# Batch 0's second half: sums a unit later, the next pair's clusters with precedence, its preparation two units sooner

## The chip, the cores and the metric

The kernel runs on one core of a Trainium2 chip. Its engines work side by side, each through a queue of its own: TensorE (PE in the profile, PEld for its weight loads), VectorE (DVE), ScalarE (ACT), GpSimd (POOL) and the sync engine (SP), which issues most transfers. The metric is the device time of one execution in microseconds; the reference point is the median of three runs.

## What is computed

Attention over clusters, followed by a feed-forward layer with a squared ReLU. B, H, S, D = 4, 8, 768, 64; 16 clusters; the model width is 512, the hidden width 2048.

```python
q_assign = np.argmax(np.einsum('bhsd,hcd->bhsc', q_n, c_n), axis=-1)
k_assign = np.argmax(np.einsum('bhsd,hcd->bhsc', k_n, c_n), axis=-1)
mask = q_assign[:, :, :, None] == k_assign[:, :, None, :]
scores = scale * np.matmul(q, k.transpose(0, 1, 3, 2))
scores = np.where(mask, scores, -1000000000.0)
...
attn = attn / (np.sum(attn, axis=-1, keepdims=True) + 1e-09)
return np.matmul(attn, v)
# then, with the heads side by side as x (3072 x 512):
h = x @ w_in
r = np.maximum(h, 0.0)
return ((r * r) @ w_out)
```

A query attends to the keys of its own cluster only.

## The kernel before

**Units.** Heads go in pairs (16 pairs, four in a batch), queries in two halves of 384, keys in blocks of 128. A unit is one pair, one half and two key blocks; there are 96. Batch 0 takes its four pairs with the first half of the queries (units 0 to 11) and then the same four pairs with the second half (units 12 to 23, three for a pair). From unit 24 on, each pair of batches 1 to 3 has its six units in one piece. `TWOS` is 12, `HP` is 4, `NCH` is 6.

**A unit.** `scores` multiplies keys and queries into two PSUM tiles `sc`, and for batch 0 adds a penalty from the one-hot clusters; ScalarE takes the exponential (line 466). From pair 4 on, VectorE masks the result by comparing cluster numbers `qid` and `ids` (line 470). `times_v` multiplies by the values into `av`, for two units together at odd units. In batch 0's first half TensorE itself sums the exponentials; in the second half and later GpSimd adds them up in `acc` (lines 480, 482).

**The end of a pair and half.** `add_up` multiplies `acc` by a constant on TensorE into `sm` (a tile of the pool `ps_f`, which has two banks and serves logits, turned logits, sums and the feed-forward alike), takes the reciprocal `r` on VectorE (line 551), sends it to DRAM as `far_r` and brings it back spread over the partitions as `rb`, all through the sync queue. One unit later `finish` multiplies `av` by `rb` into `xT` (line 570) and so releases the `av` bank; there are two of these.

**Preparation.** `prep(pair)` is a list of steps, three of which are taken in each unit. For pairs 4 and up it is: bring the words of q and k back turned (`turn_words`), split the next pair's words (`split_words`, two calls), `logits`, `route` (which turns the logits into `lt` on TensorE and finds each row's cluster on VectorE, lines 340 to 349), and `spread`, which sends the cluster numbers to all partitions. For pair 4 the two halves of its own words are split by the main loop, in units 12 and 15; its preparation begins in unit 18 (line 764), and its first scores are in unit 24.

**Beside it.** In units 0 to 23 `round_weights` rounds 32 tiles of the feed-forward weights in pieces that ScalarE, VectorE and GpSimd take in turn (lines 150 to 166): one tile in most units, two in every third. Four staging tiles `w_raw` are loaded through the sync queue as they come free. The feed-forward of batch 0 (`ffn`, lines 584 and 597) is cut into single matmuls that fill TensorE between the attention's own; it begins at the end of the first half. The feed-forward of batches 1 to 3 runs after unit 95.

**Order.** The program is traced unit by unit; each engine's instructions are put in order by the time at which a model finds them ready and by precedence, where earlier traced goes first. `tc.high_priority(offset=n)` treats what it encloses as if it had been traced n places earlier. `tc.issue_after` puts instructions behind one that is named. On the chip each engine then works through its written order.

Of the kernel before, what the change touches and what calls it, by code (L numbers as in the profile page):

```python
# [25 lines left out]
def kernel(  # L26
# [14 lines left out]
    NCH = S // P  # L41
# [4 lines left out]
    HP = H // 2  # L46
# [54 lines left out]
    def load_qk(pair):  # L101
        if pair >= NG:
            return
        b, hp = divmod(pair, HP)
        raw[pair] = []
        for name, src in (("q_raw", q), ("k_raw", k)):
            t = loads.tile([P, NCH, 2 * D], F32, name=name, tag="qk")
            for e in range(2):
                (nc.scalar if pair == 0 and e else nc.sync).dma_start(
                    t[:, :, D * e : D * (e + 1)],  # L110
                    src[b, 2 * hp + e].rearrange("(p j) d -> p j d", p=P),
                )
            raw[pair].append(t)

    def load_v(pair):
        b, hp = divmod(pair, HP)
        raw_v[pair] = loads_v.tile([P, 2, NCH, D], F32, name="v_raw")
        nc.sync.dma_start(
            raw_v[pair], v[b, 2 * hp : 2 * hp + 2].rearrange("h (p j) d -> p h j d", p=P)
        )  # L120
# [16 lines left out]
    def load_weights(i):  # L137
        raw_w[i] = wstage.tile([P, NW, 2], U32, name="w_raw")
        nc.sync.dma_start(raw_w[i], weights[i][1])
# [129 lines left out]
    def split_words(pair, which):  # L269
        if which == 0:  # L270
            words[pair] = dram.tile([2 * NCH, P, 2, 2 * D], U16, name="words")
        flat = loads.tile([P, NCH, 2, 2 * D], U16, name="flat", tag="qk")
        src = raw[pair][which].bitcast(U16).rearrange("p c (d two) -> p c two d", two=2)
        half = NCH // 2
        with tc.issue_after(last_exp[0]):
            for cols in (slice(0, half), slice(half, NCH)):
                nc.scalar.copy(out=flat[:, cols], in_=src[:, cols])
        nc.sync.dma_start(
            words[pair][NCH * which : NCH * (which + 1)].rearrange("c p two d -> p c two d"),
            flat,  # L280
        )
        if which == 1:
            raw.pop(pair)
            load_qk(pair + 1)
# [22 lines left out]
        nc.scalar.copy(out=lgs[pair], in_=lg)  # L307

    def route(pair):
        with tc.high_priority(offset=2000) if pair < HP else ExitStack():  # L310
            number(pair)

    def number(pair):
# [95 lines left out]
    def prep(pair):  # L409
        if pair < HP:  # L410
            return [
                lambda: turn(pair, 0), lambda: turn(pair, 1), lambda: turn(pair, 2),
                lambda: logits(pair), lambda: route(pair),
                lambda: turn_onehot(pair, 0), lambda: turn_onehot(pair, 1),
            ]

        split = [lambda i=i: split_words(pair + 1, i) for i in range(2 if pair + 1 < NG else 0)]
        first, second = split or (None, None)
        return [
            lambda: turn_words(pair), None, None, first, None, None,  # L420
            lambda: logits(pair), None, lambda: route(pair), second, None, None,
            None, None, lambda: spread(pair),
        ]
# [9 lines left out]
    def first_half(pair, h):  # L433
        return pair < HP and h == 0
# [63 lines left out]
    def wide(pair, h):  # L498

        return (pair, h) == (HP - 1, 0)  # L500

    def times_v(pair, h, c):
        if c == 0:
            av[pair, h] = ps_av.tile([P, TB], F32, name="av", tag="av")
            if first_half(pair, h):
                n = TB if wide(pair, h) else TB // 2
                sums[pair, h] = ps_av.tile([P, n], F32, name="sm", tag="av")
        t = ex.pop((pair, h, c))
        products = [
            dict(  # L510
                out=av[pair, h][D * e : D * (e + 1)], lhsT=raw_v[pair][:, e, c + i],
                rhs=t[:, 2 * i + e], start=(c + i == 0), stop=(c + i == NCH - 1),
            )
            for i in range(2) for e in range(2)
        ]
        if first_half(pair, h):
            for i in range(2):
                one = [
                    ones_products(
                        sums[pair, h], wide(pair, h), e, t[:, 2 * i + e], c + i == 0, c + i == NCH - 1  # L520
                    )
                    for e in range(2)
                ]
                products += [p for both in zip(*one) for p in both]
        together(products, 4000)
# [211 lines left out]
    TWOS = HP * NCH // 2  # L737
# [17 lines left out]
    def behind_first(u, what=last_logits):  # L755
        return tc.issue_after(what[0]) if u == 0 else ExitStack()

    def next_pair(u):

        pair, h, c = units[u]  # L760
        if c == 0 and pair + 1 < NG and h == 0 and (pair + 1) not in qkT:
            if pair + 1 < HP or pair >= HP:
                return pair + 1
        if c == 0 and h == 1 and pair == HP - 2:
            return HP
        return None

# [10 lines left out]
    for _ in range(AHEAD):  # L778
        load_weights(next(loaded))
    added = []  # L780
    v_next = 0

    def ends(halves):
        for pair, h in halves:
            b, hp = divmod(pair, HP)
            finish(pair, h)
            if hp == HP - 1 and (b, h) in PLAIN:
                fill.append(ffn(b, h))

    for u in range(len(units) + 2):  # L790
        if u < len(units):
            pair, h, c = units[u]
            if (p := next_pair(u)) is not None:
                ahead.extend(prep(p))
            if u in (HP * NCH // 2, HP * NCH // 2 + 3):

                split_words(HP, int(u > HP * NCH // 2))
            if c == 0 and u + 3 < len(units) and units[u + 3][0] not in raw_v:
                load_v(units[u + 3][0])

            with behind_first(u):
                scores(pair, h, c)

        ends(added)
        added.clear()
        if u < TWOS:
            ready = u - 1
        elif u == TWOS or u % 2 or u >= len(units):
            ready = u
        complete = []  # L810
        while v_next < min(ready, len(units)):
            pair, h, c = units[v_next]
            times_v(pair, h, c)
            v_next += 1
            if c == NCH - 2:
                complete.append((pair, h))
        for pair, h in complete:
            with tc.high_priority(offset=1000) if pair < HP else ExitStack():
                add_up(pair, h)
            if h == 1:  # L820
                for d in (qkT, ids, qid):
                    d.pop(pair)
            if h == 1 or pair < HP:
                raw_v.pop(pair)
            if wide(pair, h):
                with tc.high_priority(offset=1000):
                    ends([(pair, h)])
            else:
                added.append((pair, h))

        rounding += 4
        while rounding >= 3:
            rounding -= 3
            i = next(to_round, None)
            if i is not None:
                with tc.issue_after(last_exp[0]):
                    round_weights(i)
                if (i := next(loaded, None)) is not None:
                    load_weights(i)
            elif not later:  # L840
                early.close()
                for name, bufs in (("xT", 5), ("out", 2)):
                    later[name] = keep.enter_context(
                        tc.tile_pool(name=name + "_late", bufs=bufs, side="right",
                                     reuse_waits="tile")
                    )
        share = 0
        if u % 2 == 0 or not TWOS < u < len(units):
            n = 2 if TWOS < u < len(units) else 1
            share = max(0, left[0] - RESERVE) * sum(map(density, range(u, u + n)))  # L850
            share //= max(1, sum(map(density, range(u, ENDS))))
        goal = left[0] - share

        for i in range(3):
            if i == 2:
                fill_steps(share * 2 // 3)
            if ahead:
                with behind_first(u, masked if i else last_logits):
                    (ahead.pop(0) or int)()
        fill_steps(left[0] - goal)  # L860
# [235 lines left out]
```

## Time and profile before

| what | value |
|---|---|
| time, median of three runs | 995.92 us (994.25 to 997.6) |
| profiled span | 992.5 us |
| attention with batch 0's feed-forward | up to some 550 us |
| feed-forward of batches 1 to 3 | the rest |
| TensorE busy from 73.7 to 182 us (units 12 to 25) | 97.6 us |
| VectorE, ScalarE, GpSimd busy in the same stretch | 74.4, 59.9, 64.6 us |
| mean granted TensorE clock | 0.995 of full speed |

A row of the timeline has the start in us, the duration in us (of a merged run of instructions the stretch it covers), the engine, the line of the kernel, the operation, the tiles written and read, shapes, and the count; in brackets stands how long the engine was idle before it and what ended that. A line such as L91 is a helper's (`together`), so the tile tells which product it is: `sc` scores, `av` values, `sm` sums, `lg` logits, `lt` turned logits, `ph` and `po` feed-forward. Matmul ends are modelled, so durations of groups are taken from start to start.

### The profile page before, as it was taken

How to read it: one execution, taken by the hardware profiler on the slowest of the kernel's cores; microseconds unless marked ns; L12 is line 12 of the kernel's file. 1: busy time of each engine (PE TensorE's matmuls, PEld its weight loads, DVE VectorE, ACT ScalarE, POOL GpSimd, SP SyncE). 2: the span in 40 equal slices, each digit the busy share in tenths (PEclk: the TensorE clock that was granted, in tenths of full speed). 3: DMA queues.
4: the chain of work that ended last, by engine and by line, in shares of the span. 5: the costliest groups of instructions: out<-in, count | busy, mean ns of one | idle time of the engine just before them, and what ended most of it. 6: DMA issues, size and time to landing. Idle time of an engine off the chain costs nothing.

```text
span 992.5 us, 12014 instructions
## 1 busy us (share of the span) xinstructions
PE 963.3 (97%) x4455; PEld 552.3 (56%) x4455; DVE 563.4 (57%) x913; ACT 315.5 (32%) x510; POOL 374.4 (38%) x277
## 2 busy tenths in 40 slices
PE   7998989999999999999899999999999999999997
PEld 4543434343444444444343555888655888556886
DVE  5767584765566656666765855533465531556331
ACT  5885664444445455554232111000111000111000
POOL 1336574555565565655556332001331002231000
PEclk9999998999999999999999999999999999999999
DMA  9654655345554445544310000000000000000000
GB/s 259 192 179 143 180 167 120 96 107 129 123 128 123 113 115 111 138 106 99 88 38 17 20 0 1 1 22 22 21 1 0 11 22 27 7 0 1 22 22 24
DMA packets 127576, 74.32 MB, mean 75 GB/s; under 512 B 90907, under 2 KB 118935, under 8 KB 127511
## 3 DMA queue, kind: packets, MB, share of 16 engines
q1 hardware_dynamic: 125798, 73.06, 28.0%
q8 instruction: 37, 0.61, 0.2%
q10 hardware_dynamic: 1712, 0.43, 0.2%
q14 instruction: 29, 0.23, 0.1%
HBM read 48.07 MB, written 15.86 MB: 64 GB/s over the span
## 4 chain that ended last, share of the span: by engine, by line
PE 79%; DVE 5%; issue 5%; DMA 5%; POOL 3%; SPq 1%; ACT 1%; ACTq 0%; POOLq 0%; DVEq 0%
PE bank L707 22%; PE bank L676 22%; PE po L597 7%; PE ph L584 6%; PE sc L91 5%; PE sc L94 5%; PE av L91 4%; PE av L94 4%; DMA rb<-far_r 2%; POOL acc L482 2%; POOL w_in L166 1%; DVE ex L470 1%; PE sm L91 1%; DVE w_raw L162 1%; DVE r L551 1%
## 5 line engine op out<-in xcount | busy, mean ns | idle before, releaser
L482 POOL TENSOR_TENSOR acc<-acc,ex 128x768 f32<-128x768 f32 x112 | 205.0, 1830 | 124.9 <-DVE ex L470 99.7
L470 DVE SCALAR_TENSOR_TENSOR ex<-qid,ids,sc 128x384 f32<-128x384 bf16 x288 | 157.6, 607 | 62.2 <-ACT sc L466 40.7
L466 ACT ACTIVATE sc<-sc 128x768 f32<-128x768 f32 x144 | 108.6, 793 | 162.7 <-PE sc L94 136.7
L94 PE MATMUL sc<-qkT 64*128 64x384 f32 x576 | 153.1, 504 | 0.9
L94 PE MATMUL av<-ex,v_raw 128*64 128x384 f32 x576 | 136.8, 494 | 0.0
L646 DVE TENSOR_TENSOR g<-bank,g 128x384 f32<-128x384 f32 x144 | 77.8, 555 | 81.6 <-PE bank L676 80.5
L665 POOL TENSOR_TENSOR w_s<-w_in 128x256 f32<-128x256 f32 x24 | 18.2, 760 | 278.5 <-PE bank L707 162.0
L584 PE MATMUL ph<-xT,w_in 128*128 128x384 f32 x256 | 94.6, 511 | 0.7 <-DVE xT L570 0.7
L707 PE MATMUL bank<-w_out,g 128*128 128x256 f32 x432 | 95.2, 379 | 0.0
L91 PE MATMUL sc<-qkT 64*128 64x384 f32 x192 | 87.5, 536 | 5.4 <-DVE ex L470 5.4
L597 PE MATMUL po<-w_out,gT 128*128 128x512 f32 x192 | 91.6, 609 | 0.0
L707 PEld LDWEIGHTS bank<-w_out,g 128*128 128x128 f32 x432 | 82.1, 190 | 11.8
L646 DVE TENSOR_TENSOR osb<-bank,osb 128x256 f32<-128x256 f32 x54 | 22.1, 423 | 107.6 <-PE bank L707 102.3
L94 PEld LDWEIGHTS sc<-qkT 64*128 64x128 f32 x576 | 65.2, 186 | 28.6 <-issue 6.2
L91 PE MATMUL av<-ex,v_raw 128*64 128x384 f32 x192 | 81.0, 504 | 0.0
L480 POOL TENSOR_TENSOR acc<-ex 128x768 f32<-128x768 f32 x28 | 50.9, 1820 | 51.0 <-DVE ex L470 36.6
L676 PE MATMUL bank<-xT,w_in 128*128 128x384 f32 x192 | 69.9, 487 | 0.0
L676 PE MATMUL bank<-x_t,w_s 128*128 128x384 f32 x192 | 69.8, 486 | 0.0
L676 PE MATMUL bank<-xT,w_s 128*128 128x384 f32 x192 | 69.8, 486 | 0.0
L584 PEld LDWEIGHTS ph<-xT,w_in 128*128 128x128 f32 x256 | 46.5, 193 | 40.7 <-issue 14.5
L94 PEld LDWEIGHTS av<-ex,v_raw 128*64 128x64 f32 x576 | 49.6, 137 | 34.9 <-issue 34.8
L707 PE MATMUL bank<-w_t,g 128*128 128x256 f32 x288 | 65.1, 379 | 0.0
(128 smaller groups left out, 1221.6 us busy)
## 6 DMA issues: line engine op xcount, KB each, us to landing
words<-flat SPq DMA_DIRECT2D x24, 384.0 KB
w_raw<-in_moe_w_in_dram SPq DMA_DIRECT2D x16, 512.0 KB
w_raw<-in_moe_w_out_dram SPq DMA_DIRECT2D x16, 512.0 KB
v_raw<-in_v_dram SPq DMA_DIRECT2D x20, 384.0 KB
q_raw<-in_q_dram SPq DMA_DIRECT2D x31, 192.0 KB
k_raw<-in_k_dram SPq DMA_DIRECT2D x31, 192.0 KB
rb<-far_r SPq DMA_DIRECT2D x62, 96.0 KB
out_dram<-osb SPq DMA_DIRECT2D x23, 256.0 KB
```

The source lines that it names most:

```text
L91: last = nc.tensor.matmul(**next(products))
L94: last = nc.tensor.matmul(**product)
L466: last_exp[0] = nc.scalar.activation(out=t[:, 2 * i : 2 * i + 2] if pair < HP else src, in_=src, func=ACT.Exp, scale=SCALE).ins
L470: nc.vector.scalar_tensor_tensor(out=t[:, 2 * i + e], in0=qid[pair][1][:, h, e], scalar=ids[pair][:, ch % NB, 2 + ch // NB, e : e + 1], in ...
L480: nc.gpsimd.tensor_tensor(out=acc[pair, h], in0=t[:, 0:2], in1=t[:, 2:4], op=ALU.add)
L482: nc.gpsimd.tensor_tensor(out=acc[pair, h], in0=acc[pair, h], in1=t[:, 2 * i : 2 * i + 2], op=ALU.add)
L584: nc.tensor.matmul(ph, lhsT=w_in[:, kk, f * P : (f + 1) * P], rhs=xT[b, h][:, kk], start=(kk == 0), stop=(kk == KT - 1),)
L597: nc.tensor.matmul(po, lhsT=gT[f][:, i * P : (i + 1) * P], rhs=w_out[:, f], start=(f == 0), stop=(f == FT - 1),)
L646: nc.vector.tensor_tensor(out=out, in0=bank, in1=to, op=ALU.add)
L665: nc.gpsimd.tensor_tensor(out=s1, in0=a[1][0], in1=a[1][1], op=ALU.add)
L676: nc.tensor.matmul(bank, lhsT=operands[j][0][:, kk], rhs=operands[j][1][:, kk], start=(kk == 0), stop=(kk == H2 - 1),)
L707: nc.tensor.matmul(bank, lhsT=operands[j][0][:, f], rhs=operands[j][1][:, f], start=(f == 0), stop=(f == F2 - 1),)
```

## The change

Three things are changed in units 12 to 25. The sums of the second half come a unit later: a pair that is complete goes onto the list `late` and is added up in the next unit, without the lead of 1000 in precedence that only first halves keep. For pair 3 the condition `u < HP * NCH` no longer holds when it is complete (unit 25), so it changes only its precedence. Pair 4's clusters (`route`) get the lead of 2000 that batch 0's pairs have. And pair 4's preparation begins in unit 16 instead of 18, for which the second half of its words is split in unit 14 instead of 15. The purpose is that the sums are asked for when what they need is there, and that pair 4's clusters are out of the way of them.

```diff
     def route(pair):
-        with tc.high_priority(offset=2000) if pair < HP else ExitStack():
+        with tc.high_priority(offset=2000) if pair <= HP else ExitStack():
             number(pair)
...
-        if c == 0 and h == 1 and pair == HP - 2:
+        if u == TWOS + 4:
             return HP
...
+    late = []
...
-            if u in (HP * NCH // 2, HP * NCH // 2 + 3):
-
-                split_words(HP, int(u > HP * NCH // 2))
+            if u in (TWOS, TWOS + 2):
+
+                split_words(HP, int(u > TWOS))
...
-        complete = []
+
+        complete, late = late, []
         while v_next < min(ready, len(units)):
             pair, h, c = units[v_next]
             times_v(pair, h, c)
             v_next += 1
             if c == NCH - 2:
-                complete.append((pair, h))
+                (late if u < HP * NCH and h else complete).append((pair, h))
         for pair, h in complete:
-            with tc.high_priority(offset=1000) if pair < HP else ExitStack():
+            with tc.high_priority(offset=1000) if first_half(pair, h) else ExitStack():
                 add_up(pair, h)
```

## The prediction

> **What bounds the kernel now.** I read the page first, for the share of each engine and for the chain that ended last.
>
> ```profile
> PE 963.3 (97%) x4455; PEld 552.3 (56%) x4455; DVE 563.4 (57%) x913; ACT 315.5 (32%) x510; POOL 374.4 (38%) x277
> ...
> PE 79%; DVE 5%; issue 5%; DMA 5%; POOL 3%; SPq 1%; ACT 1%; ACTq 0%; POOLq 0%; DVEq 0%
> ```
>
> TensorE (PE) is busy 963.3 of 992.5 us and carries 79% of the chain. The change alters no matmul count, so it can only give back TensorE idle time, some 29 us in all, and time that its matmuls take at a reduced clock. Next, the waits of TensorE (columns: total us, times, longest us).
>
> ```profile
> PE sm L91 <- POOL acc L482: 5.6, 2, 3.3
> PE sc L91 <- DVE ex L470: 5.4, 5, 2.5
> PE sm L91 <- DVE best L341: 5.1, 1, 5.1
> ```
>
> Two of the longest belong to `sm`, the column sums that the change moves. To place them I numbered the units by their exponentials (two `ex` activations each; unit 12, the first of batch 0's second half, has its scores at 73.8, unit 24 at 169.3 us) and asked for TensorE's timeline there.
>
> ```profile
> 96.56 0.35 PE L91 MATMUL sm<-acc,ups 128*32 128x192 f32 x1 [3.29 <-POOL acc L482]
> ...
> 149.72 0.50 PE L91 MATMUL sm<-acc,ups 128*32 128x192 f32 x1 [5.15 <-DVE best L341]
> ```
>
> The first is pair 0's sum in unit 15, the second pair 2's in unit 21; pairs 1 and 3 (127.56, 173.71 us) did not wait. Then the stages around them (after the stretch: its length, busy us and counts of PE, PEld, DVE, ACT, POOL; granted clock, DMA share, GB/s).
>
> ```profile
> 93.30:96.50 3.20, 0.00 (x0) 0.00 (x0) 3.20 (x2) 1.31 (x3) 3.12 (x3) 1.00 0.71 225
> 96.50:102.60 6.10, 6.04 (x26) 2.74 (x26) 3.58 (x4) 1.01 (x2) 2.71 (x3) 0.72 0.44 154
> ...
> 144.60:149.70 5.10, 0.00 (x0) 0.01 (x1) 5.00 (x6) 0.00 (x0) 4.44 (x3) 0.93 0.86 248
> 149.70:156.00 6.30, 6.28 (x22) 2.19 (x22) 2.44 (x4) 0.00 (x0) 0.17 (x1) 0.52 0.64 155
> ```
>
> TensorE stands still, then comes back at 0.72 and 0.52 of its clock. VectorE (DVE) is full in both gaps, with weight rounding. Its timeline ahead of the second shows what `best` was late for:
>
> ```profile
> 144.92 1.39 DVE L159 TENSOR_SCALAR w_out<-w_out 128x512 uint32<-128x512 uint32 x1
> 146.23 2.29 DVE L162 SCALAR_TENSOR_TENSOR w_raw<-w_raw 128x512 uint32<-128x512 uint32 x1
> 148.44 0.54 DVE L340 TENSOR_REDUCE mx<-lt 128x24 f32<-128x384 f32 x1
> 149.02 0.56 DVE L341 TENSOR_TENSOR best<-lt,mx 128x384 bf16<-128x384 f32 x1
> ```
>
> Pair 4's transposed logits `lt` were in PSUM by 142.29 us (the row at 141.80, 0.49 long). VectorE reached them 6.15 us later, after roundings; `lt` held one of the two `ps_f` banks until line 341 had read it, and `sm` waited for that bank.
>
> **What the Trainium skill says.** "TensorE: Matmul & The Clock Gate", Part 1, states that after an idle window of about 3.4 us the array runs at half clock until it has been busy about as long. The trace agrees in kind: 3.29 us idle is followed by 0.72 over 6.1 us, 5.15 us by 0.52 over 6.3 us. "SBUF — State Buffer", section "SBUF: two separate sides", calls the port pair of VectorE and GpSimd (POOL) an exclusive lock, held for a whole instruction. Line 155's rounding agrees: 0.41 us alone (124.91), 1.65 us begun during GpSimd's additions (86.64). "Perfetto Trace Analysis", "Tensor Engine Instruction", says that VectorE and ScalarE queues are strict FIFO; the 6.15 us agree. So a place in the order decides what waits.
>
> **The change part by part.**
>
> *Sums a unit later (lines 810 to 819).* Pairs 0, 1, 2 move from units 15, 19, 21 to 16, 20, 22 and lose the lead of 1000; pair 3 keeps unit 25 and loses only the lead. Pair 0's `acc` was complete at 96.5 us, after GpSimd had done a rounding (90.93, 1.41) and the last two additions (4.20). One unit is about 8 us here (95.5 us over 12 units), against 3.29 us missing. In the gap TensorE has six `ph` matmuls, unit 15's scores and two sets of `av` ready, so this wait goes: 3.29 us. The clock loss behind it: the six `ph` took 3.46 us from 97.02 to 100.48, the same six took 2.14 from 135.16 to 137.30, so 1.32; the scores took 2.13 (100.48 to 102.61) against 1.82 (82.77 to 84.59), so 0.31. Together **4.92 us**. Other merit: `round_weights` handles two weights in units 14, 17, 20 and one otherwise; the sums that waited followed a double (units 14 and 20), and the new places 16, 20, 22 follow units with one.
>
> *Precedence and earlier preparation (lines 310, 764, 795).* Pair 4's preparation starts in unit 16, its logits and clusters come in unit 18 instead of 20, with a lead of 2000 that puts `lt` and the four cluster operations (0.54 + 0.56 + 0.68 + 0.55 = 2.33 us) ahead of roundings that are not yet issued. The wait at 149.72 is thus removed twice: the bank is free two units before, and the sum asks a unit later. 5.15 us, plus the clock: `sm` 0.80 (149.72 to 150.52) against 0.46 (127.56 to 128.02), four `ph` 2.86 against 1.43, eight `av` 2.61 (153.38 to 155.99) against 1.44 (142.22 to 143.66): 0.34 + 1.43 + 1.17 = 2.94. Together **8.09 us**.
>
> *Word splits in 12 and 14.* The second split (two copies of 0.81 us on ScalarE) comes a unit sooner, with pair 4's transposing DMA and pair 5's loads. I cost them at nothing: ScalarE is busy 60 us of the 108 from 73.7 to 182, and the words wait for the sync queue (copied by 94.2, issued 101.88) rather than the reverse. The transposing DMA was issued at 109.17, in unit 16, and unit 18's logits would follow scores at 119.0; the issue takes 5.08 us, which leaves some 4 us, more if the words leave earlier.
>
> *What it adds.* (a) `lt` on TensorE waits for the copy `lgs`, behind roundings on ScalarE. Queued behind `lt` are all later matmuls. For pair 4 the copy ended at 138.51, 3.28 us after the logits; the other `lt` waits of the page total 1.0 us in 3. Bound 0 to 3.3; I take 0.6. (b) VectorE's roundings queue behind clusters that wait for `lt`: GpSimd and `w_raw` loads behind them, hidden by the four staging buffers. (c) `sm` now holds its bank until the reciprocal (1.34 us) without a lead; `ph` waits for that bank. Bound 0 to the 6.15 us that `lt` met; I take 0.5. (d) Pair 3's sum (0.46 us) no longer stands ahead of unit 25's scores, which waited 1.34 us for VectorE's `ex`: +0.46. (e) `finish` moves a unit back, and `av` of two pairs on waits for its bank. From `sm` to the end of `xT` it took 11.3 us for pair 0 (96.56 to 107.85) and 12.4 for pair 2 (149.72 to 162.12). The room is 22.6 us for pair 0 (scores of unit 16 at 107.2 to `av` at 129.8) and 20.5 for pair 2 (157.8 to 178.3): nothing.
>
> Sum: 995.92 - 4.92 - 8.09 + 0.6 + 0.5 + 0.46 = **984.5 us**. Units after 24 have the same order as traced, and since TensorE is the bound there too, what is saved before 170 us reaches the end.
>
> **The rivals.**
> *One wait comes back.* ScalarE, VectorE and GpSimd must do the same in 13 us less; the lock makes VectorE and GpSimd (74 and 65 us busy of 108) partly exclusive. If one late sum, or an `lt` behind the copy, still idles TensorE as long as a removed wait: 984.5 + 4.9 = 989.4, or + 8.1 = 992.6. For it: a late reciprocal can sit behind roundings just as `best` did. Against: pair 1's and pair 3's sums met no such wait.
> *The waits only change their name.* Both return at the same size, as head-of-line waits on `lgs`, an `r` or a `qkT` transfer: 984.5 + 13.0 = 997.5 at most, about no change. For it: the lead can put `lt` too early. Against: the first two pieces each act without the other.
> *Slower.* The sums lose their lead on VectorE and the sync queue. That queue waited 44.0 us in 12 waits (longest 9.8) for GpSimd to release `w_raw`, from 60 to 260 us. Two such waits in a sum's chain make 12.4 + 19.6 = 32.0, beyond the 22.6 of room by 9.4; with a clock loss like 2.94 a pair costs 12.3. With two pairs so: 984.5 + 24.6 = 1009; one alone gives 997. Or two sums in four hold the bank as `lt` did, with the clock: 984.5 + 16.2 = 1000.7. Against: in before, the requests for `far_r` at 100.63 and 130.78 left within 0.7 us of the reciprocal's end.
>
> **How the numbers follow.** Forecast 0.58, one wait back 0.24, changed name 0.07, slower 0.11. The low end: (a) to (d) at nothing and the 1.34 us of unit 25 gone too gives 981.6, or 981.0 with the run's own spread of 0.2%. The high end takes in most of the first rival: 992. Outside are the second and third rival and a little of the first, about 2 in 10. Faster by over 0.3% means under 992.9: 0.82; within: 0.06; slower: 0.12.
>
> **What would show it.** `sm` rows from 90 to 150 us with no idle ahead of them; no stretch under 0.9 of the clock between 84 and 160 us; unit 24's first scores near 157 instead of 169.3; `mx` of pair 4 within about 2 us of its `lt`; the sum of TensorE's waits smaller by about 8. Wrong would be: a new idle of over 3 us ahead of `lt`, `lg`, `ph` or `av` in that stretch, or the gain at unit 24 lost again by unit 95.

## The result, and the profile after

The changed kernel takes 983.96 us (median of four runs, 982.73 to 985.26) against 995.09 us for the kernel before beside it: ratio 0.9887, 95% interval 0.9859 to 0.9916. The forecast was 984.5 us. The sum came out right, but two of its terms did not, and they happened to cancel.

The page of the changed kernel, engine shares and chain:

```profile
PE 962.6 (98%) x4455; PEld 552.8 (56%) x4455; DVE 562.4 (57%) x913; ACT 315.4 (32%) x510; POOL 376.9 (38%) x277
...
PE 81%; DVE 6%; DMA 5%; issue 3%; ACT 1%; POOL 1%; SPq 1%; ACTq 0%; DVEq 0%; POOLq 0%
```

TensorE does the same work (962.6 us against 963.3) in a span of 983.0 instead of 992.5 us. TensorE's waits (total us, times, longest us):

```profile
PE sc L91 <- DVE ex L470: 2.6, 3, 1.1
PE sm L91 <- POOL acc L482: 2.3, 1, 2.3
PE ph L584 <- DVE best L341: 2.3, 1, 2.3
```

Of the two `sm <- acc` waits one is left, the 2.3 us after unit 95 that the kernel before has too (at 545.41 us there). `sm <- best` is gone from the list, but `best` is not: `ph` now waits for it. TensorE's timeline shows the places:

```profile
102.84 0.35 PE L91 MATMUL sm<-acc,ups 128*32 128x192 f32 x1
...
125.17 0.55 PE L317 MATMUL lt<-ident,lgs 128*128 128x128 f32 x3 [0.45 <-ACT gT L591]
...
130.73 0.88 PE L584 MATMUL ph<-xT,w_in 128*128 128x384 f32 x2 [2.28 <-DVE best L341]
```

Pair 0's sum at 102.84 has no bracket: it did not wait. At 130.73 the same bank is missing as before, held by `lt`, and this time a feed-forward matmul is the victim. The stretches before and after that row (columns as in the prediction):

```profile
126.00:130.73 4.73, 2.46 (x12) 0.78 (x11) 4.66 (x5) 1.28 (x3) 4.65 (x3) 1.00 0.85 258
130.73:136.42 5.69, 5.69 (x22) 2.12 (x22) 1.99 (x3) 0.00 (x0) 2.02 (x2) 0.70 0.60 156
```

VectorE and GpSimd are busy nearly all through the gap, and TensorE comes back at 0.70 of its clock. VectorE's timeline says with what:

```profile
127.22 2.31 DVE L162 SCALAR_TENSOR_TENSOR w_raw<-w_raw 128x512 uint32<-128x512 uint32 x1
129.45 0.55 DVE L340 TENSOR_REDUCE mx<-lt 128x24 f32<-128x384 f32 x1
130.03 0.56 DVE L341 TENSOR_TENSOR best<-lt,mx 128x384 bf16<-128x384 f32 x1
```

`lt` was complete at 125.72 us (125.17 + 0.55); the clusters still stood behind the roundings of one weight tile and began 3.7 us later, at 129.45.

To see where time went I cut each profiled span at the start of the first exponential of units 12, 15 and 24 and at the first matmul of batch 1's feed-forward. All columns are in us; "timed" is the ratio of the times to those of the kernel before, run beside each kernel, with its 95% interval.

| kernel | to unit 12 | 12 to 15 | 15 to 24 | 24 to feed-forward | rest | timed |
|---|---|---|---|---|---|---|
| before | 75.64 | 26.98 | 67.75 | 381.61 | 440.52 | |
| changed | 76.56 | 21.74 | 64.76 | 379.57 | 440.37 | 0.9887 (0.9859 to 0.9916) |
| e1 lead alone | 75.71 | 21.01 | 63.19 | 381.15 | 440.24 | 0.9911 (0.9892 to 0.9929) |
| e2 list and lead | 76.53 | 21.02 | 64.40 | 379.23 | 440.42 | 0.9898 (0.9879 to 0.9918) |
| e3 early preparation | 76.60 | 28.94 | 63.94 | 382.47 | 440.45 | 0.9976 (0.9959 to 0.9993) |
| e4 precedence | 75.71 | 26.72 | 65.76 | 383.04 | 440.27 | 0.9966 (0.9950 to 0.9982) |
| e5 changed, lead restored | 76.81 | 25.05 | 62.36 | 385.82 | 440.26 | 0.9967 (0.9954 to 0.9979) |
| e6 changed, no precedence | 75.63 | 21.87 | 64.74 | 378.94 | 440.42 | 0.9904 (0.9879 to 0.9929) |
| e7 changed, `lt` copied out | 81.54 | 21.41 | 63.78 | 380.48 | 440.24 | 0.9911 (0.9878 to 0.9943) |
| e8 changed, rounding behind | 75.66 | 21.39 | 60.84 | 379.16 | 440.45 | 0.9857 (0.9831 to 0.9882) |
| e9 changed, no list | 75.79 | 21.39 | 63.46 | 383.67 | 440.19 | 0.9929 (0.9905 to 0.9954) |
| e10 e9, rounding behind | 75.57 | 21.71 | 60.77 | 383.46 | 440.29 | 0.9931 (0.9907 to 0.9956) |
| e11 before, doubles moved | 79.41 | 30.32 | 62.16 | 381.05 | 440.33 | 0.9997 (0.9986 to 1.0009) |
| e12 e2, rounding behind | 75.61 | 21.01 | 63.19 | 379.13 | 440.16 | 0.9898 (0.9880 to 0.9916) |

The first column is start-up, which no edit but e11's touches; it too varies between executions (e7). Timed values of separate executions spread by some us, so small differences are read from the stretches and the waits in them. The stretches are of one execution each, and their clock differs: e3 and e5 turn out to have the same instructions in the same order on all five engines, and still the stretch from 12 to 15 took 28.94 us in one, 6.83 us of it at half the clock and with 1.1 us more of waiting for `xT`, and 25.05 us in the other, at full clock (last section). A difference counts here where a wait in the trace accounts for it.

### The profile page after: what moved, and what is told of

It reads as the page before. It is cut to its first block, busy times and chain, and to the rows that moved or that the text cites. A ratio compares the mean times of both kernels' runs of the same rounds, so it can differ in the third digit from the quotient of the medians.

```text
span 983.0 us, 12011 instructions
## 1 busy us (share of the span) xinstructions
PE 962.6 (98%) x4455; PEld 552.8 (56%) x4455; DVE 562.4 (57%) x913; ACT 315.4 (32%) x510; POOL 376.9 (38%) x277
## 4 chain that ended last, share of the span: by engine, by line
PE 81%; DVE 6%; DMA 5%; issue 3%; ACT 1%; POOL 1%; SPq 1%; ACTq 0%; DVEq 0%; POOLq 0%
PE bank L707 22%; PE bank L676 22%; PE po L597 7%; PE ph L584 6%; PE sc L91 6%; PE sc L94 5%; PE av L91 5%; PE av L94 4%; DMA rb<-far_r 3%; DVE w_raw L162 1%; DVE r L551 1%; PE sm L91 1%; DVE ex L470 1%; DMA far_r<-r 1%; POOL w_in L166 1%
## 5 line engine op out<-in xcount | busy, mean ns | idle before, releaser
L482 POOL TENSOR_TENSOR acc<-acc,ex 128x768 f32<-128x768 f32 x112 | 207.1, 1849 | 115.0 <-DVE ex L470 98.4
L584 PE MATMUL ph<-xT,w_in 128*128 128x384 f32 x256 | 91.8, 498 | 3.3 <-DVE best L341 2.3
L707 PE MATMUL bank<-w_t,g_s 128*128 128x256 f32 x288 | 65.1, 379 | 0.0
```

What stands on the lines that cost most here:

```text
L482: nc.gpsimd.tensor_tensor(out=acc[pair, h], in0=acc[pair, h], in1=t[:, 2 * i : 2 * i + 2], op=ALU.add)
L584: nc.tensor.matmul(ph, lhsT=w_in[:, kk, f * P : (f + 1) * P], rhs=xT[b, h][:, kk], start=(kk == 0), stop=(kk == KT - 1),)
L707: nc.tensor.matmul(bank, lhsT=operands[j][0][:, f], rhs=operands[j][1][:, f], start=(f == 0), stop=(f == F2 - 1),)
```

## The experiments

Theory A is the prediction's: the unit of delay takes away pair 0's wait, and delay, precedence and early preparation together take away pair 2's. Theory B arose on comparing the written order of the instructions: losing the lead of 1000 already moves the sums that far, and the list adds nothing.

**e1, the lost lead alone.**

```diff
-            with tc.high_priority(offset=1000) if pair < HP else ExitStack():
+            with tc.high_priority(offset=1000) if first_half(pair, h) else ExitStack():
```

> The kernel before with one edit: the sums of pairs 0 to 3 in the second half lose their lead of 1000; no list of late sums, no earlier preparation, no precedence of the clusters. Theory A (as predicted: the unit of delay is what helps): pair 0's sum is still asked for in unit 15, so a good part of the 3.29 us stays; time within 3 us of before. Theory B (the lead was the fault, the delay adds nothing): the written order already puts the sum behind unit 15's scores and values, some 4 us later, when acc is complete; the wait before pair 0's sum is 0 and its clock loss gone, about 5 us; pair 4's lt still holds its bank, so the second stall stays, at 3 to 8 us with its clock loss, perhaps under the name of ph. Time 5 to 7 us under before.

985.08 against 994.06 us. Theory A, which had the time within 3 us of before, is out. TensorE's timeline of this kernel:

```profile
99.45 0.35 PE L91 MATMUL sm<-acc,ups 128*32 128x192 f32 x1
...
132.22 0.51 PE L91 MATMUL lg<-qkT,cnT 128*32 128x384 f32 x1 [3.29 <-DVE r L551]
```

Pair 0's sum, still of unit 15 but now behind that unit's scores and values, does not wait. Theory B holds for the first stall: one line gives all of it (26.98 to 21.01 us). The gain, 9.0 us against the 5 to 7 that B expected, is larger because the second stall went as well: pair 2's sum (145.07 us) now stands behind the values of unit 20, and line 341 had read `lt` by 144.38. In exchange pair 1's sum holds a bank until its reciprocal, which without a lead stands behind a rounding (the reciprocal starts at 130.82, the sum at 126.58), and `lg` waits 3.29 us for it. That is item (c) of the prediction.

**e2, list and lost lead.** On the kernel before:

```diff
+        complete, late = late, []
...
-                complete.append((pair, h))
+                (late if u < HP * NCH and h else complete).append((pair, h))
...
-            with tc.high_priority(offset=1000) if pair < HP else ExitStack():
+            with tc.high_priority(offset=1000) if first_half(pair, h) else ExitStack():
```

> The kernel before with the sums' part of the change alone: list of late sums and lost lead. Theory A: 4.9 us for pair 0's sum, and the second stall also shrinks since pair 2's sum asks a unit later: 8 or more us under before. Theory B: as without the list, 5 to 7 us under before; what waits for the bank that lt holds is now a ph, because it is lt and not the sum that sets that wait.

983.63 us, 10.4 us under before. That is the size of theory A and not of B, but e1 without the list is only 1.5 us behind, which the intervals don't separate; nor do they separate e2 from the whole change (0.9887). From unit 12 to 24 it is no better than e1 (85.42 against 84.20 us). From unit 24 on it is 1.92 us shorter. What waits for `lt`'s bank is still pair 2's sum, 2.00 us at 147.14, and not a `ph` as B had it.

**e3, early preparation alone.** On the kernel before:

```diff
-        if c == 0 and h == 1 and pair == HP - 2:
+        if u == TWOS + 4:
             return HP
...
-            if u in (HP * NCH // 2, HP * NCH // 2 + 3):
+            if u in (TWOS, TWOS + 2):
```

> The kernel before with pair 4's preparation in unit 16 and its second split in unit 14 alone. Both theories: pair 0's wait of 3.3 us stays, with about 1.6 us of clock loss. Theory A: lt and its clusters are out of the way before pair 2's sum, second stall gone, 8 us under before. Theory B: lt moves two units up but its clusters stay behind the same kind of roundings on VectorE, so a bank wait of 2 to 3 us plus clock loss stays, under the name of a ph or a sum: 2 to 4 us under before.

991.67 us, 2.4 under before, as theory B had it and not A (8 us): pair 0's wait stays (2.92 us), and at 137.12 us `ph` waits 1.89 us for `best`.

**e4, precedence alone.** On the kernel before:

```diff
-        with tc.high_priority(offset=2000) if pair < HP else ExitStack():
+        with tc.high_priority(offset=2000) if pair <= HP else ExitStack():
             number(pair)
```

> The kernel before with the lead of 2000 for pair 4's clusters alone. In the written order the clusters stand one rounding of three operations sooner on VectorE. Theory A: the second stall falls from 5.15 us to under 2 us, and with less than 3 us idle its clock loss mostly too: 5 to 8 us under before; pair 0's wait stays. Theory B: lt is also written sooner (after one ph tile's quarter of a unit), so it waits for VectorE as long as before: under 3 us gained.

990.99 us, 3.1 under before, just beyond B's limit of 3 and short of A's 5 to 8. The second stall is now 3.48 us of `ph` on `best` instead of 5.15 us of `sm`: the clusters pass the roundings of one weight tile (`mx` starts at 144.30 instead of 148.44), `lt` comes sooner too (139.67 instead of 141.80), and the bank still waits.

**e5, the changed kernel with its lead restored.**

```diff
-            with tc.high_priority(offset=1000) if first_half(pair, h) else ExitStack():
+            with tc.high_priority(offset=1000) if pair < HP else ExitStack():
```

> The changed kernel with the lead of 1000 given back to the late sums; the list of late sums, the early preparation and the precedence stay. Theory A (the unit of delay is what helps): the sums are still traced a unit later, so the time stays within 2 us of the changed kernel. Theory B (the lost lead alone): a lead of 1000 places is far more than a unit, so the written order puts pair 0's sum back into unit 14's ph matmuls; wait of 3 us on acc with 1.6 us of clock loss returns, and the time is that of early preparation alone, 990 to 992.

989.27 against 992.76 us. One row of TensorE's timeline is enough:

```profile
97.44 0.35 PE L91 MATMUL sm<-acc,ups 128*32 128x192 f32 x1 [2.94 <-POOL acc L482]
```

With the lead, the list of late sums is void: all five engines have the instructions of e3 in the order of e3, pair 0's sum is back among unit 14's `ph` matmuls and waits. The time is just under the 990 to 992 of theory B; theory A falls for the first stall.

**e6, the changed kernel without precedence.**

```diff
-        with tc.high_priority(offset=2000) if pair <= HP else ExitStack():
+        with tc.high_priority(offset=2000) if pair < HP else ExitStack():
             number(pair)
```

> The changed kernel without the lead of 2000 for pair 4's clusters. Theory A (the lead takes the clusters past roundings): mx of pair 4 comes later and the stall at unit 20 grows by 2 us or more, 2 to 5 us over the changed kernel. Theory B (with preparation two units sooner nothing stands there that the lead could pass): all five engines have the same instructions in the same order as the changed kernel, so the same waits and the same time within noise.

984.57 us. All five engines have the same instructions in the same order as in the changed kernel, and the stretch from unit 12 to 24 agrees to 0.1 us. The precedence, worth 3.1 us alone (e4), does nothing in this change. The pair also shows what a profile's single values are worth: the wait of `sc` on `ex` near 470 us is 0.87 us in the one and 2.49 us in the other.

**e7, `lt` copied out of its bank.**

```diff
+        if pair == HP:
+            nc.scalar.copy(out=src, in_=lt.rearrange("p i n -> p (i n)"))
+            lt = src.rearrange("p (i n) -> p i n", i=NB)
```

> The changed kernel; for pair 4 alone ScalarE copies the turned logits out of their PSUM bank (into the buffer of lgs, free by then) and VectorE reads the copy, so the bank no longer waits for VectorE. One more ScalarE operation of about 0.5 us. If the stall left at unit 20 is the bank that lt holds until VectorE has read it: the wait of 2.28 us of ph on best and most of the about 3 us of clock loss go, 3 to 5 us under the changed kernel. Rival: the stall is VectorE and GpSimd being late with everything there, so that another wait (ph, sm or ex) of about the same size takes its place; no gain.

984.23 us, the same as e6 beside it. The wait on `best` is gone, as it should be, and TensorE's timeline shows its successor (line numbers are three higher here):

```profile
141.61 2.85 PE L587 MATMUL ph<-xT,w_in 128*128 128x384 f32 x8 [2.17 <-DVE r L554]
```

Pair 1's sum now holds the bank until its reciprocal, which stands behind the late clusters. The rival was right: freeing one bank does not help while VectorE's order stays. The 12 to 24 stretch is 1.4 us shorter than e6's; e6 has 3.41 us at half the clock behind its wait and e7 none.

**e8, one rounding behind the clusters.** `clusters[0]` is the last cluster operation of `number`.

```diff
-                with tc.issue_after(last_exp[0]):
+                with tc.issue_after(last_exp[0]), (
+                    tc.issue_after(clusters[0]) if u == TWOS + 7 else ExitStack()
+                ):
                     round_weights(i)
```

> The changed kernel; VectorE's three roundings of the weight tile of unit 19 are put behind pair 4's clusters in its order (about 4 us of roundings passed), all else as it is. If one rounding ahead of the clusters is what keeps the bank: mx starts within 0.5 us of lt, the wait of 2.28 us on best is 0 and the clock stays up, 4 to 5 us under the changed kernel. Rival (VectorE and GpSimd as a whole are the limit of units 18 to 22): the roundings left behind delay acc, and a wait of sm on acc of 2 us or more takes its place, no gain.

979.34 us (978.16 to 980.14), with e6 at 984.57 (980.80 to 985.13) in the same set of runs: 5.2 us less, and the best of all. VectorE's timeline (line numbers one higher):

```profile
121.98 2.32 DVE L162 SCALAR_TENSOR_TENSOR w_raw<-w_raw 128x512 uint32<-128x512 uint32 x1
124.53 0.56 DVE L341 TENSOR_REDUCE mx<-lt 128x24 f32<-128x384 f32 x1 [0.23 <-PE lt L318]
125.12 0.56 DVE L342 TENSOR_TENSOR best<-lt,mx 128x384 bf16<-128x384 f32 x1
...
128.36 1.45 DVE L155 TENSOR_SCALAR w_out<-w_out 128x512 f32<-128x512 f32 x1
```

VectorE is idle for 0.23 us and takes `lt` as it comes; the rounding follows at 128.36. No wait on `best`, and the stretch from 15 to 24 falls from 64.74 (e6) to 60.84 us: 3.9 us, close to the 2.28 us of wait and 1.7 us of clock loss that were left. TensorE, ScalarE and GpSimd have the same order as in the changed kernel, so the roundings of one tile ahead of the clusters were the cause of the stall that the change left.

**e9, the changed kernel without the list.**

```diff
-        complete, late = late, []
+        complete = []
...
-                (late if u < HP * NCH and h else complete).append((pair, h))
+                complete.append((pair, h))
```

> The changed kernel without the list of late sums: the lead stays away, preparation stays early. In TensorE's written order the sums stand behind the scores and values of their old units, 15, 19 and 21. Theory A (the unit of delay matters): a wait on acc of 1 us or more returns ahead of pair 0's sum, and the time is 3 us or more over the changed kernel. Theory B (the lead alone): no wait on acc there, pair 0's stretch from unit 12 to unit 15 within 1 us of the 21.7 of the changed kernel; time within 3 us of it. A cost of up to 2 us in unit 19 is possible in both, since pair 1's sum then holds a bank while lt holds the other.

986.68 us, 7.2 under before. Pair 0's stretch is 21.39 us, without a wait on `acc`: theory B. But up to the feed-forward it is 4.1 us slower from unit 24 on than the changed kernel, which neither theory had.

**e10, e9 with one rounding behind the clusters.** The diffs of e9 and e8 together.

> As the run before, with VectorE's roundings of unit 19 behind pair 4's clusters (the edit that took the changed kernel to 979.3 us). If the list of late sums is of no use: 978 to 981 us. If it is what keeps pair 1's sum and lt from holding both banks at once: a wait of 2 to 4 us of ph on r or best around unit 19, 982 to 986 us.

985.94 us. From unit 12 to 24 it equals e8 (82.48 against 82.23 us), so that the bank conflict of the expectation did not occur; the whole loss is later. TensorE's timeline, unit 25:

```profile
164.18 0.56 PE L91 MATMUL sc<-qkT 64*128 64x384 f32 x1 [2.17 <-DVE ex L471]
```

The other kernels without a working list have this wait too (1.34 us before, 2.19 in e1, 1.45 in e3, 1.33 in e4, 1.99 in e5, 2.18 in e9), with one exception, e11 below, and no kernel in which the list works has it. The list moves pair 2's sum into unit 22, and the model that orders the instructions then fills TensorE differently: with it 18 of the `ph` matmuls stand between the scores of units 23 and 24, without it they stand ahead of unit 23. In the changed kernel the exponentials of 23 and 24 start at 153.72 and 163.06, in e1 at 156.17 and 159.91. VectorE thus gets some 9 us instead of 4 for the last roundings before unit 24's masks. The exception fits: in e11 the two exponentials lie 7.46 us apart as well, in all others without a working list 3.7 to 3.8. This account is read from the traces; no run changes the spacing alone. In the stretch from 24 on, the six kernels in which the list works took 378.94 to 380.48 us and the eight others 381.05 to 385.82. Not all of that is the list's. Of the 4.1 us of e9, 2.2 are this wait, up to 1.7 are 3.41 us at half the clock behind it (from 168.48 us; in e10 from 165.87, in e1 none), and 1.4 are later waits on `ex`; against that the changed kernel lost 1.2 us of clock at the end of the attention. The later waits (the one near 470 us is 2.48 here, 0.87 in e8) vary under one order, as e6 shows, and they are not put down to the list.

**e11, the kernel before with its double roundings moved.**

```diff
-    rounding = 0
+    rounding = 1
```

> The kernel before; the count that spaces the weight roundings starts at 1 instead of 0, so that units 13, 16, 19, 22 round two weight tiles and units 14, 17, 20, 23 one. All sums stay where they are, with their lead. Theory of the prediction (pair 0's acc is late because the double roundings of unit 14 hold up GpSimd): the wait ahead of pair 0's sum falls from 3.29 us to 1.5 or less. Rival (the sum is asked for before GpSimd could be done in any case: after unit 14's exponential at 89.3 us two additions of 1.9 us must follow two of unit 13): the wait stays at 2.5 us or more.

993.35 against 993.88 us: no difference. GpSimd's and TensorE's timelines:

```profile
94.42 1.41 POOL L166 TENSOR_TENSOR w_out<-w_out,w_raw 128x512 int32<-128x512 int32 x1 [0.97 <-DVE w_raw L162]
96.79 1.39 POOL L166 TENSOR_TENSOR w_out<-w_out,w_raw 128x512 int32<-128x512 int32 x1 [0.97 <-DVE w_out L159]
98.15 4.18 POOL L482 TENSOR_TENSOR acc<-acc,ex 128x768 f32<-128x768 f32 x2
```

```profile
102.39 0.53 PE L91 MATMUL sm<-acc,ups 128*32 128x192 f32 x1 [5.66 <-POOL acc L482]
```

The wait grew to 5.66 us. What stands ahead of the last two additions on GpSimd are the roundings of unit 13: one before (90.93 us), two here. Those of unit 14 come behind the additions (96.47 and 98.89 us before), so the double in unit 14 was not the fault; it was to ask while additions and roundings were still queued. For pair 2 the double of unit 20 does seem to count: with one tile in that unit the sum waits 1.73 us for `best` instead of 5.15 (the other doubles moved too, so this is not shown alone). With their clock losses the two make the stretch to unit 15 3.34 us longer and that from 15 to 24 5.59 shorter; in the timed values no gain is left.

**e12, e2 with one rounding behind the clusters.** On e2:

```diff
+                    tc.issue_after(clusters[0]) if u == TWOS + 9 else ExitStack()
```

> The kernel before with the sums' part of the change alone (list and lost lead, as in an earlier run at 983.6 us) and VectorE's roundings of unit 21 behind pair 4's clusters; preparation stays in unit 18 and the clusters have no lead. If the early preparation is not needed once the clusters pass the rounding: the wait of 2.0 us of pair 2's sum on best goes and the time is 979 to 982 us. If it is needed: the 0.65 us of lg on r and others grow, 983 or more.

982.36 us (980.89 to 987.28), between the two expectations; its ratio of 0.9898 is that of e2. The wait on `best` only fell from 2.0 to 1.42 us and that of `lg` on `r` rose from 0.65 to 1.10. The timelines of VectorE and TensorE (line numbers one higher) show why:

```profile
144.31 0.56 DVE L571 SCALAR_TENSOR_TENSOR xT<-av,rb 128x384 f32<-128x384 f32 x1 [3.94 <-DMA rb<-far_r]
144.79 0.55 DVE L341 TENSOR_REDUCE mx<-lt 128x24 f32<-128x384 f32 x1
...
146.07 0.32 PE L91 MATMUL sm<-acc,ups 128*32 128x192 f32 x1 [1.42 <-DVE best L342]
```

`lt` was complete at 137.82 us, and VectorE stood idle for 3.94 us: in its order the clusters stand behind `xT`, which waits for `rb` to come back from DRAM. In e2 it is the same (3.25 us idle). So here it is a transfer and no longer a rounding that keeps the bank. The stretch from 15 to 24 is 63.19 us, 2.35 more than e8's, with no reduced clock in either; TensorE's waits in it are 3.03 us against 0.46. So once the clusters pass the roundings, the early preparation is worth some 2 us, because it takes them out from behind that transfer as well; the timed intervals of e8 and e12 overlap, and it is the stretch that says so.

## Why the prediction was right, and where it was not

The profiled spans differ by 9.5 us: +0.92 before unit 12, -5.24 to unit 15, -2.99 to unit 24, -2.04 to the feed-forward, -0.15 after.

- **Pair 0's stall, 4.92 us.** Right in size: with its own 0.46 us, which move into the next stretch, the sum should shorten this one by 5.38, and it measured 5.24. The clock loss went with the wait. The step behind it was wrong: it set the unit of delay, about 8 us, against the 3.29 us missing. e1 and e5 show that it is the lost lead that does it, with or without the list, and e11 that the double of unit 14 is not the cause; the double of unit 20 may lengthen pair 2's wait, as the prediction's "other merit" had it.
- **Pair 2's stall, "removed twice", 8.09 us.** This step failed. What is left is 2.28 us of `ph` on `best`, and a clock loss of 1.73 us (eight `av` 2.76 us, from 131.54 to 134.30, against 1.34 from 145.70 to 147.04; the next scores 2.12 against 1.81, so 1.42 + 0.31): 4.0 us, so that 4.1 were gained. The bank was rightly named as the cause; that the lead of 2000 takes the clusters past the roundings was not true, since with the early preparation it changes no instruction's place (e6). "Removed twice" took `sm` for the only one who asks: the sum moved, and a `ph` asked for the bank instead. e8 shows the term at its size, once the roundings of one tile are really passed.
- **(a) `lt` behind the copy, 0.6 us:** 0.45 us measured, but not behind the copy, which was done by 120.54. The row at 125.17 names line 591, where ScalarE reads a `ph` out of its bank: `lt` too waited for a bank, and the size is right by luck. **(c) bank held until the reciprocal, 0.5:** nothing in the changed kernel, but 3.29 us in e1 and 2.17 in e7, inside the bound.
- **(d) unit 25's scores, +0.46 us.** Wrong sign: the wait of 1.34 us vanished, and the stretch after unit 24 got 2.04 us shorter, in part through the later waits on `ex`, which vary. e10 against e8 shows the list as the cause, by the traces through the place of the `ph` matmuls. That is what the delay is good for; the prediction let this wait go only in its low end, without a reason.
- **(b) and (e), at nothing.** (b) was not put to the test in the changed kernel, where the clusters passed no rounding; in e8, where they do, VectorE waited 0.23 us for `lt`. (e) was right: `av` waits for no bank. Pair 0's chain from `sm` to `xT` took 13.84 us (102.84 to 116.68), 2.5 more than before, inside the room of 22.6.
- **The rivals.** "One wait comes back" is half of what happened: the bank wait returned under the name of `ph`, at about half its size (4.0 of 8.1 us with the clock). "Slower" did not occur, nor did both waits return under another name. By stretches the sum stands for 5.38 us less to unit 15, 6.53 less to unit 24 (8.09, less the 0.46 of pair 0's sum, 0.6 and 0.5) and 0.46 more after; the spans show 5.24, 2.99 and 2.04 less. 3.5 us too many in the second and 2.5 too few in the third leave a sum that is close by luck, not by insight.
- **What would show it.** Two of the five signs came: the `sm` rows have no idle time ahead of them, and TensorE's waits from 60 us on fell from 16.9 to 8.4 us in sum. The clock fell to 0.50 from 131.54 us on, unit 24's first scores came at 162.10 and not near 157, and `mx` came 3.7 us after `lt` and not within 2. All three point to pair 2's term.

Undoing single parts puts it thus: losing the lead carries most of the gain (e1 0.9911; with the lead restored, e5, 0.9967), the list a wait of 1.3 to 2.2 us after unit 24 and in some executions up to 1.7 us of clock behind it, early preparation little by itself and about 2 us once the clusters pass the roundings of one tile, precedence 3 us alone and nothing beside the early preparation.

## What to carry to other kernels

When an edit moves work "later" and also drops its precedence, compare the written order of the instructions for each half of the edit before giving either the credit: one of them may be void. A wait for a buffer is a fact about who holds it and in what queue the holder's reader stands; moving the one who asks only picks another victim, and letting the reader pass the roundings of one tile ahead of it (e8) was worth 5 us. A reader can also stand behind an instruction that itself waits, as in e12; then an idle engine keeps the buffer. In a sum of estimates, look at each stretch afterwards even where the total fits.

## What the runs showed of the hardware

The clock's price of an idle stretch doesn't follow its length alone. 3.29 us idle ahead of `sm` in the kernel before were followed by a clock of 0.72 for 6.1 us, while in e1 the eight `lg` behind an idle time of the same 3.29 us took 0.78 us (132.22 to 133.00), as in the kernel before without a wait (134.38 to 135.16). In the changed kernel 2.28 us were enough for 0.70 over 5.69 us. At the end of the attention 2.32 us idle cost nothing before (fourteen `po` in 6.11 us, 545.87 to 551.98) and 2.33 us cost 1.16 us after (7.27 us, 535.36 to 542.63).

The place in time decides. In these profiles the clock falls to 0.50 for one or two pieces of 3.41 us at a time (the last stretch, at the end of the kernel, can have another length), and within a profile the starts lie whole multiples of 3.413 us apart: in the kernel before at 97.75, 148.95 and 992.04 us, the last two 15 and 262 multiples after the first. That makes a grid. The rows below show pairs of neighbouring pieces of it (columns as in the prediction): the kernel before at pair 0's stall and at the end of the attention, then the changed kernel, then e1, whose grid is set by its only reduced stretch, from 980.46 us.

```profile
94.34:97.75 3.41, 1.19 (x10) 0.64 (x11) 3.41 (x3) 0.27 (x1) 3.38 (x2) 1.00 0.53 169
97.75:101.16 3.41, 3.41 (x7) 1.52 (x7) 2.33 (x3) 0.54 (x2) 1.46 (x2) 0.50 0.40 154
...
541.48:544.89 3.41, 1.61 (x10) 0.49 (x6) 0.05 (x1) 0.00 (x0) 3.14 (x2) 1.00 0.00 0
544.89:548.31 3.42, 2.90 (x14) 1.40 (x15) 1.36 (x1) 0.00 (x0) 3.42 (x6) 1.00 0.01 2
...
128.13:131.54 3.41, 1.13 (x5) 0.30 (x2) 3.34 (x4) 0.00 (x0) 3.33 (x3) 1.00 0.90 255
131.54:134.95 3.41, 3.41 (x11) 1.28 (x12) 1.18 (x3) 0.00 (x0) 1.21 (x1) 0.50 0.28 48
...
127.14:130.55 3.41, 1.78 (x12) 0.79 (x12) 3.41 (x2) 2.50 (x5) 3.13 (x2) 1.00 0.89 269
130.55:133.96 3.41, 1.74 (x11) 0.83 (x12) 3.38 (x4) 2.54 (x5) 2.98 (x2) 1.00 0.16 19
```

A piece with TensorE busy for 1.19 or 1.13 us, that is 65% and 67% idle, is followed by half the clock; with 1.61 us (53% idle) it is not. In e1 the 3.29 us are split by a border of the grid into two pieces of about half each, and cost nothing. In the fourteen profiles, from 70 us on, no piece at full clock that was at most 53% idle was followed by half the clock, and each one that was 60% idle or more was; in between both occur. The busy times rest on modelled matmul ends, so these shares are rough. The grid lies differently in each execution, which is why e3 and e5, with one order and almost the same wait of pair 0's sum (2.92 and 2.94 us), paid 6.83 us at half the clock and nothing. So a clock loss measured once, as those of 1.63 and 2.94 us in the prediction, is the loss of that execution.

"TensorE: Matmul & The Clock Gate", Part 1, of the Trainium skill calls the window free-running, which fits one length with two prices; its condition of one idle window of about 3.4 us does not fit a loss after 2.28 us, and there the measurement decides.
